# Blocks 3 to 8 of the first network in three pairs, seven products for each gate and value term, sums kept in PSUM

## The chip, the cores and the metric

One core of one Trainium2 chip runs the whole program. The metric is device microseconds of one execution, the median of several. PE (TensorE) does the matmuls, DVE (VectorE), ACT (ScalarE) and POOL (GpSimd) the elementwise work; SP and ACT issue the DMAs. PSUM has eight banks of 128x512 fp32; "bank" always means one of these.

## The reference

Attention in chunks of 64 positions for 8 batches, 8 heads and 576 positions of width 64 gives x of 4608 tokens by 512. Two networks follow:

```python
s = scale * q_c @ k_c.T ; p = exp(s - max(s)) ; x = (p / (sum(p) + 1e-9)) @ v_c
xn = x / sqrt(mean(x * x) + 1e-6) * rms_g
y = (silu(xn @ w_gate) * (xn @ w_val)) @ w_out        # 512 -> 1536 -> 512
h = y @ w_in                                          # 512 -> 2048
out = (h * clip(h + 3, 0, 6) / 6) @ w_out2            # 2048 -> 512
```

## The kernel before

Tokens are worked in nine blocks of N = 512. Every fp32 operand is split into a high part and a remainder (fp32r), and a product of two operands is made of three matmuls (high by high, low by high, high by low). One "term" of 128 output rows over the full depth of 512 is then 12 matmuls of 128x512.

The work is under a manual schedule: each engine runs its instructions in the order in which the code issues them, and waits where a semaphore is not there yet. So an instruction that waits on DVE, ACT or POOL holds all that was issued behind it on that engine, and a DMA that waits for its buffer holds what stands behind it on SP's or ACT's queue.

First network, per block b (loop at L903): for each of the 12 tiles f of 128 hidden rows, `mm_up` makes the gate (12 matmuls, L728, bank GB), ACT makes silu from it (L911), `mm_up` makes the value (bank VB), DVE multiplies (L916), `split_act` casts the high part on ACT (`ah`, L781) and takes the remainder on POOL (`al`, L782), and `mm_down_a` of the tile before (12 matmuls, L752, L753, L755) adds to four banks of y. So the PE order is gate, value, down, 36 matmuls a tile and 432 a block. At the block's end `x_split` makes XH (ACT, L717) and XL (DVE and POOL, L719) of the next block, the last `mm_down_a` runs, and `y_store` (L788 to L790) puts y into DRAM.

Between these steps two hooks put other work, by the position hk (three a tile). `att_hook` runs the attention of block b+1: two units (class Pair) of 256 tokens each with their transposes (L581, L582), scores (L594), max, subtract, exp, sum, normalization on POOL (L630), and so on, then `halve` and `rms` (L692 to L707: squares' mean by two matmuls, square root on ACT with a table load, RECIPROCAL and four multiplies on DVE). `prep_hook` runs `Stash.step`: in each of blocks 1 to 8 it prepares one of eight parts of the second network's weights (raw loads, bit operations L238 to L247 and sums L288 to L291 on DVE, high parts on ACT, remainders on POOL, sixteen 256 KB stores from ACT's queue).

The second network takes block 0 by `mm_up` and blocks 1 to 8 in four pairs by the Strassen-Winograd scheme: seven block products in place of eight, each a `product` of six matmuls (L739) with weight operands streamed from the stash (`Stream.ahead`, L349, 512 KB each) and token operands made by `x_fill` (differences L954, casts L959, remainders L962). Its sums are made outside PSUM: ACT copies a product out (L1027), DVE adds the others (L1030 to L1052).

The change touches the first network's block loop, the hooks, `Stash.step`, `rms`, `x_split` and `product`, and adds an operand preparation and a loader.

## Time and profile before

| what | value |
|---|---|
| median of 3 runs | 1764.86 us (1764.82 to 1765.2) |
| profiled execution, span from first to last instruction | 1762.2 us |
| median less that span | 2.7 us |
| PE busy | 1720.4 us, 98% |
| DVE, ACT, POOL busy | 51%, 37%, 28% |
| matmuls of 128x512 | 7168 |

The page gives the span of the profiled execution and no separate total for it; the runs agree within 0.4 us, so the span and the median differ by what lies around the span. A matmul's busy time overlaps its neighbour's, so the pitch of a run of matmuls is taken from the chain, where pieces stand end to end.

### The profile page before, as it was taken

Reading aid. Unit: us, or ns where it says so; the run is one execution under the profiler, and the core shown is the slowest. Engines: PE = TensorE matmul, PEld = TensorE weight load, DVE = VectorE, ACT = ScalarE, POOL = GpSimd, SP = SyncE. Lnnn points to the kernel's source line nnn. Section 1 sums busy time; section 2 is a strip of 40 time slices with the busy share of each in tenths; the row PEclk is TensorE's granted clock in tenths of the full one; section 3 lists DMA queues with packets and bytes.
Section 4 is the critical chain, followed back from the end, with each engine's and each line's share of the span. In section 5 each row is a group of like instructions: output and inputs, shape, how many; then the busy total and the mean of one; then the engine's idle time right before and its main releaser. Section 6 shows DMA issues by size and latency. Waiting matters only on the chain.

```text
span 1762.2 us, 24680 instructions
## 1 busy us (share of the span) xinstructions
PE 1720.4 (98%) x9664; PEld 1416.8 (80%) x9664; DVE 893.4 (51%) x1202; ACT 644.5 (37%) x971; POOL 488.8 (28%) x360
## 2 busy tenths in 40 slices
PE   5789999999999999999999999999999999999999
PEld 4568788888888888888888888888888888888887
DVE  7996544545455444545542243545554554465440
ACT  5554334333343334334332133333333333343332
POOL 2321332333233232332323232112321321151123
PEclk8889999999999999999999999999999999999999
DMA  9832342423424242343317354544244334424420
GB/s 253 236 85 36 97 108 75 108 64 91 108 76 117 64 106 71 97 108 77 92 51 263 140 204 147 175 143 144 72 167 139 125 111 137 138 92 146 142 67 29
DMA packets 273589, 207.17 MB, mean 118 GB/s; under 512 B 196289, under 2 KB 233153, under 8 KB 273345
## 3 DMA queue, kind: packets, MB, share of 16 engines
q1 hardware_dynamic: 240704, 163.65, 32.4%
q10 hardware_dynamic: 32768, 41.95, 7.2%
q8 instruction: 76, 1.25, 0.3%
q14 instruction: 41, 0.33, 0.1%
HBM read 161.48 MB, written 44.04 MB: 117 GB/s over the span
## 4 chain that ended last, share of the span: by engine, by line
PE 93%; DVE 4%; SPq 1%; POOL 1%; ACT 1%; issue 0%; DMA 0%; DVEq 0%; ACTq 0%
PE PS L728 34%; PE PS L739 17%; PE PS L764 7%; PE PS L761 7%; PE PS L760 7%; PE PS L752 6%; PE PS L753 5%; PE PS L755 5%; PE PS L654 1%; PE PS L594 1%; DVE w L195 1%; PE PS L636 1%; DVE wtmp L175 1%; POOL al L782 1%; DVE wtmp L171 1%; DVE wraw L179 1%
## 5 line engine op out<-in xcount | busy, mean ns | idle before, releaser
L782 POOL TENSOR_TENSOR al<-sg,ah 128x512 fp32r<-128x512 f32 x156 | 215.5, 1381 | 988.6 <-ACT ah L781 685.9
L728 PE MATMUL PS<-XH,w 128*128 128x512 f32 x1728 | 432.3, 393 | 9.3 <-DVE sg L916 4.6
L728 PEld LDWEIGHTS PS<-XH,w 128*128 128x128 f32 x1728 | 326.7, 189 | 79.1 <-DVE sg L916 5.3
L739 PE MATMUL PS<-xo,wq 128*128 128x512 f32 x1344 | 309.2, 389 | 0.0
L739 PEld LDWEIGHTS PS<-xo,wq 128*128 128x128 f32 x1344 | 252.3, 188 | 52.4
L728 PE MATMUL PS<-XL,w 128*128 128x512 f32 x864 | 232.3, 391 | 0.0
L760 PE MATMUL PS<-w,ah 128*128 128x512 f32 x576 | 224.1, 389 | 0.0
L761 PE MATMUL PS<-w,ah 128*128 128x512 f32 x576 | 224.1, 389 | 0.0
L916 DVE TENSOR_TENSOR sg<-sg,PS 128x512 f32<-128x512 f32 x108 | 74.0, 685 | 283.6 <-PE PS L728 274.3
L781 ACT CAST ah<-sg 128x512 fp32r<-128x512 f32 x156 | 96.8, 621 | 272.5 <-DVE sg L916 242.4
L728 PEld LDWEIGHTS PS<-XL,w 128*128 128x128 f32 x864 | 163.0, 189 | 34.7 <-POOL XL L520 0.6
L752 PE MATMUL PS<-ah,w 128*128 128x512 f32 x432 | 174.4, 404 | 1.3 <-ACT ah L781 1.3
L753 PE MATMUL PS<-ah,w 128*128 128x512 f32 x432 | 169.4, 392 | 0.0
L764 PE MATMUL PS<-w,al 128*128 128x512 f32 x576 | 154.3, 389 | 0.0
L911 ACT ACTIVATE sg<-PS 128x512 f32<-128x512 f32 x108 | 64.5, 597 | 227.4 <-PE PS L728 175.3
L761 PEld LDWEIGHTS PS<-w,ah 128*128 128x128 f32 x576 | 108.1, 188 | 22.5
L764 PEld LDWEIGHTS PS<-w,al 128*128 128x128 f32 x576 | 108.1, 188 | 22.4
L760 PEld LDWEIGHTS PS<-w,ah 128*128 128x128 f32 x576 | 108.1, 188 | 22.4
L755 PE MATMUL PS<-al,w 128*128 128x512 f32 x432 | 115.8, 390 | 0.0
L1030 DVE TENSOR_TENSOR u<-u,PS 128x512 f32<-128x512 f32 x32 | 22.0, 687 | 156.8 <-PE PS L739 147.7
L752 PEld LDWEIGHTS PS<-ah,w 128*128 128x128 f32 x432 | 81.5, 189 | 20.0 <-ACT ah L781 1.8
L755 PEld LDWEIGHTS PS<-al,w 128*128 128x128 f32 x432 | 81.3, 188 | 17.3 <-POOL al L782 0.3
(140 smaller groups left out, 1941.1 us busy)
## 6 DMA issues: line engine op xcount, KB each, us to landing
wq<-stash_in SPq DMA_DIRECT2D x152, 512.0 KB, 3.7
yd<-yst SPq DMA_DIRECT2D x18, 512.0 KB, 3.3
sraw<-in_moe_w_in_dram ACTq DMA_DIRECT2D x16, 512.0 KB, 4.9
stash_in<-slo ACTq DMA_DIRECT2D x32, 256.0 KB, 2.7
sraw<-in_moe_w_out_dram ACTq DMA_DIRECT2D x16, 512.0 KB, 5.9
w<-stash_out SPq DMA_DIRECT2D x16, 512.0 KB, 5.1
x<-yd SPq DMA_DIRECT2D x16, 512.0 KB, 5.9
out_dram<-ost SPq DMA_DIRECT2D x16, 512.0 KB, 2.9
```

Source lines behind the costliest of these rows:

```text
L728: nc.tensor.matmul(ps, w(wi, c), xs[c][xi], start=(i == 0), stop=(i == n - 1))
L739: nc.tensor.matmul(PS[:, bank, :], op[:, wi, c * 128:(c + 1) * 128], x[xi][:, c, :], start=(i == 0), stop=(i == 5),)
L752: nc.tensor.matmul(ps, wm[0], a[0], start=first, stop=False)
L753: nc.tensor.matmul(ps, wm[1], a[0], start=False, stop=False)
L755: nc.tensor.matmul(PS[:, YB + m, :], w[:, 0, m * 128:(m + 1) * 128], a[1], start=False, stop=last)
L760: nc.tensor.matmul(PS[:, base + m, :], am, w[:, 0, :], start=first, stop=False)
L761: nc.tensor.matmul(PS[:, base + m, :], am, w[:, 1, :], start=False, stop=False)
L764: nc.tensor.matmul(PS[:, base + m, :], a[1][:, m * 128:(m + 1) * 128], w[:, 0, :], start=False, stop=last)
L781: nc.scalar.copy(hi, t)
L782: nc.gpsimd.tensor_tensor(lo, t, hi.bitcast(F32), op=ALU.subtract)
L911: nc.scalar.activation(s, PS[:, GB, :], AF.Silu)
L916: nc.vector.tensor_tensor(s, s, PS[:, VB, :], op=ALU.mult)
```

## The change

Blocks 0 to 2 keep the gate, value, down order. Blocks 3 to 8 become three pairs p = 0, 1, 2. In a pair, the gate and the value of hidden tiles f = 0..11 are made for both blocks together: six steps i of two tiles, seven operands for each step, each operand used for gate (m = 0) and value (m = 1) by one `product` of six matmuls. That is 84 products, 504 matmuls, where the two blocks took 576. Then 24 `mm_down_a` follow for both blocks. A "tick" is 12 matmuls' worth of steps: two products, or one `mm_down_a`; a pair has 42 and 24 ticks.

The sums of the scheme stay mostly in PSUM: a product starts on a bank that already holds a partial sum (`first=False`). Where one partial sum goes into two results, ACT copies it from bank to bank (L1176, and again at L1183 and L1192). DVE adds one product to an SBUF tile or multiplies; silu runs on ACT; POOL multiplies two of the four gate-value tiles.

Weight operands of the pairs are made once in blocks 1 and 2 by `Operands` (twelve of them, sums on DVE and POOL, high parts on ACT, seven stores of ACT's queue each) and put into DRAM, as are the w_out tiles (`keep_w`). In a pair `Loads.ahead` streams 42 operands and 12 w_out tiles, 512 KB each, six ahead, into the pool `wp`, on SP's queue. Token operands (fourteen high and low tiles) come from `x_ops`: differences and remainders on DVE, casts on ACT.

The hooks are replaced by an agenda: `at(t, fn)` puts a step at tick t. Attention units move ahead (four in each of pairs 0 and 1, none in pair 2), the eight stash parts lie within the three pairs (24 ticks each), `rms` is split into steps with the reciprocal in two halves, and the q, k, v loads are issued at most five a tick.

```diff
+STEPS_P = (
+    (0, ("turn_q",)),
+    (1, ("turn_k",)),
+    (3, ("scores", "top")),
...
+    def at(t, fn, *args, turn=2):
+        agenda[t].append((turn, lambda: fn(*args)))
...
-            t = st_p.tile([128, 1024], U32, tag="st", name="sraw")
+            t = wp.tile([128, 1024], U32, tag="w", name="sraw")
...
+        def whole(self):
+            w = [W[key] for key in self.key]
+            for k_, (t, h) in enumerate(((w[0], 0), (w[0], 1), (w[1], 1))):
+                nc.scalar.dma_start(out=self.d[:, k_, self.m], in_=t.bitcast(F32)[:, :, h * 256:(h + 1) * 256])
+            self.u = [tmp_p.tile([128, 512], F32, tag="tmp", name="ou") for _ in range(2)]
+            for u, t, e in zip(self.u, w, (nc.vector, nc.gpsimd)):
+                e.tensor_tensor(u, t[:, 0, :].bitcast(F32), t[:, 1, :].bitcast(F32), op=ALU.add)
...
+            for d, fn in ((0, self.whole), (1, self.sums), (3, self.high), (3, self.low), (4, self.keep)):
+                at(t0 + d, fn, turn=3)
...
+                    t = wp.tile([128, 2, 2, 256], F32R, tag="w", name="wo")
+                    nc.sync.dma_start(
+                        out=t.bitcast(F32).rearrange("p a b c -> p (a b c)"),
+                        in_=d1[i][:, k_].rearrange("p a b c -> p (a b c)"),
+                    )
...
+        def inv(self, h):
+            r = self.rt[:, h * 256:(h + 1) * 256]
+            nc.vector.reciprocal(r, r)
...
-    def product(bank, op, x):
+    def product(bank, op, x, first=True, last=True):
...
-                    start=(i == 0),
-                    stop=(i == 5),
+                    start=first and i == 0,
+                    stop=last and i == 5,
...
+            (4, (66, 67, 67, 67, 67, 67)),
...
+        for i, t0 in enumerate((6, 33, 58, 86, 112, 134, 153, 172)):
+            stash[i].plan(P0 + t0)
...
+            def lo(j, c, x):
+                nc.vector.tensor_tensor(XO[j][1][:, c, :], x, XO[j][0][:, c, :].bitcast(F32), op=ALU.subtract)
+
+            def diff(p, m):
+                t = tmp_p.tile([128, N], F32, tag="tmp", name="xt")
+                nc.vector.tensor_tensor(t, p, m, op=ALU.subtract)
+                return t
...
-        for b in range(NB):
+        for b in range(3):
...
+        def split_wp(t):
+            w = wp.tile([128, 2, N], F32R, tag="w", name="gs")
+            nc.scalar.copy(w[:, 0, :], t)
+            nc.gpsimd.tensor_tensor(w[:, 1, :], t, w[:, 0, :].bitcast(F32), op=ALU.subtract)
...
+                    product(bk[z][m], loads.t[key][:, m], XO[x], pr in (1, 5), pr in (2, 3, 4))
+                    if m == 1:
+                        loads.t.pop(key)
+                        loads.ahead(1)
+                    if pr == 1 and i == 0:
+                        copy(bank(1, m), bank(0, m))
...
+                    if (pr, m) == (4, 0):
+                        silu(gt(h1, 0), bank(1, 0))
+                        if i < NI:
+                            copy(bank(1, 0), bank(0, 0))
+                    elif (pr, m) == (3, 0):
+                        t = gt(h0, 1)
+                        vec(t, t, bank(4, 0), ALU.add)
+                        later = t
+                    elif (pr, m) == (4, 1):
+                        t = gt(h1, 0)
+                        vec(t, t, bank(1, 1), ALU.mult)
+                        if i < NI:
+                            copy(bank(1, 1), bank(0, 1))
+                    elif (pr, m) == (3, 1):
+                        s = hold.pop("s2")
+                        vec(s, s, bank(4, 1), ALU.add)
+                        t = gt(h0, 1)
+                        nc.gpsimd.tensor_tensor(t, t, s, op=ALU.mult)
+                    elif (pr, m) == (6, 0):
+                        copy(gt(f0, 1), bank(1, 0))
+                    elif (pr, m) == (6, 1):
+                        hold["s2"] = sg_p.tile([128, N], F32, tag="sg", name="s2")
+                        copy(hold["s2"], bank(1, 1))
+                    elif (pr, m) == (2, 0):
+                        silu(gt(f0, 0), bank(0, 0))
+                    elif (pr, m) == (2, 1):
+                        t = gt(f0, 0)
+                        vec(t, t, bank(0, 1), ALU.mult)
+                    elif (pr, m) == (7, 0):
+                        t = gt(f1, 1)
+                        copy(t, bank(1, 0))
+                        vec(t, t, bank(4, 0), ALU.add)
+                        later = t
+                    elif (pr, m) == (7, 1):
+                        s3 = tmp_p.tile([128, N], F32, tag="tmp", name="s3")
+                        copy(s3, bank(1, 1))
+                        vec(s3, s3, bank(4, 1), ALU.add)
+                        t = gt(f1, 1)
+                        nc.gpsimd.tensor_tensor(t, t, s3, op=ALU.mult)
...
+                if 0 < n < len(items) - 2:
+                    nx.append(split_wp(gt(items[n + 2][1], items[n + 2][0])))
+                mm_down_a(loads.t[p, "out", f, 0], nx[n], f == 0, f == FA - 1, yb[z])
```

Three places in the order of the engines. First DVE at the end of block 2, where the normalization of block 4 (L704 to L707, now L772 and L781) is the last before the next block. Before:

```order
L916 TENSOR_TENSOR sg<-sg,PS 128x512
L704 RECIPROCAL rt<-rt 128x512
L707 SCALAR_TENSOR_TENSOR xf<-xf,g_sb,rt 128x512 x4
L916 TENSOR_TENSOR sg<-sg,PS 128x512
L719 TENSOR_TENSOR XL<-xf,XH 128x512 x2
L789 COPY yst<-PS 128x512 x2
```

In the changed kernel, with xt and xu the token operands' differences and their split tiles, and xw the normalized block 3:

```order
L1104 TENSOR_TENSOR sg<-sg,PS 128x512
L772 RECIPROCAL rt<-rt 128x256 x2
L781 SCALAR_TENSOR_TENSOR xf<-xf,g_sb,rt 128x512 x4
L1033 TENSOR_TENSOR xt<-xf,xw 128x512
L1033 TENSOR_TENSOR xt<-xf,xt 128x512
L1029 TENSOR_TENSOR xu<-xt,xu 128x512
L1033 TENSOR_TENSOR xt<-xw,xt 128x512
L1104 TENSOR_TENSOR sg<-sg,PS 128x512
L1029 TENSOR_TENSOR xu<-xt,xu 128x512
L1033 TENSOR_TENSOR xt<-xf,xw 128x512
```

The four norms stand ahead of the block's last multiply as before; now a difference, another, a remainder and a third difference of `x_ops` stand between them and that multiply, and the two remainders XL behind it are gone.

ACT at the same place. Before:

```order
L703 ACT_TABLE_LOAD
L703 ACTIVATE rt<-PS,eps 128x512
L911 ACT_TABLE_LOAD
L911 ACTIVATE sg<-PS 128x512
L781 CAST ah<-sg 128x512
L717 CAST XH<-xf 128x512 x4
L788 COPY yst<-PS 128x512 x2
```

And in the changed kernel:

```order
L768 ACT_TABLE_LOAD
L768 ACTIVATE rt<-PS,eps 128x512
L1026 CAST xu<-xt 128x512
L1100 ACT_TABLE_LOAD
L1100 ACTIVATE sg<-PS 128x512
L1026 CAST xu<-xt 128x512
L874 CAST ah<-sg 128x512
L1026 CAST xu<-xt 128x512 x2
L881 COPY yst<-PS 128x512 x2
L1176 COPY PS<-PS 128x512 x2
```

A cast of the first difference now stands between the square root and the silu (with its table load) of the block's last tile, and after y two bank-to-bank copies (PS<-PS) follow.

PE where blocks 3 and 4 begin. Before, a block's start:

```order
L755 MATMUL PS<-al,w 128x512 x4
L728 MATMUL PS<-XH,w 128x512 x8
L728 MATMUL PS<-XL,w 128x512 x4
L728 MATMUL PS<-XH,w 128x512 x8
L728 MATMUL PS<-XL,w 128x512 x4
L728 MATMUL PS<-XH,w 128x512 x8
L728 MATMUL PS<-XL,w 128x512 x4
L728 MATMUL PS<-XH,w 128x512 x8
L728 MATMUL PS<-XL,w 128x512 x4
L594 MATMUL PS<-kT,qT 64x64 x32
L752 MATMUL PS<-ah,w 128x512
L753 MATMUL PS<-ah,w 128x512
```

And the start of the first pair, wo being the streamed operands:

```order
L848 MATMUL PS<-al,w 128x512 x4
L831 MATMUL PS<-xu,wo 128x512 x48
L655 MATMUL PS<-kT,qT 64x64 x32
L831 MATMUL PS<-xu,wo 128x512 x84
L697 MATMUL PS<-ident,p 128x128 x8
L831 MATMUL PS<-xu,wo 128x512 x24
L715 MATMUL PS<-qT,v 64x64 x32
L831 MATMUL PS<-xu,wo 128x512 x60
L655 MATMUL PS<-kT,qT 64x64 x32
```

The gate, value and down runs of the tiles give way to long runs of products, with the attention of later blocks between them; in the third pair all 504 stand in one row.

## Rows read from the trace of the kernel before

**Rows 1.** The page's head and its first part: busy us of each engine (share of the span).

```profile
span 1762.2 us, 24680 instructions
PE 1720.4 (98%) x9664; PEld 1416.8 (80%) x9664; DVE 893.4 (51%) x1202; ACT 644.5 (37%) x971; POOL 488.8 (28%) x360
```

**Rows 2.** Windows: start:end, length, busy us of five engines (instructions), PEclk, DMA share, GB/s.

```profile
64.00:66.00 2.00, 1.73 (x5) 1.39 (x6) 2.00 (x5) 1.37 (x3) 0.00 (x0) 0.68 0.90 264
70.00:123.00 53.00, 45.36 (x298) 35.31 (x297) 49.28 (x86) 28.04 (x45) 16.58 (x7) 0.90 0.58 154
176.00:182.00 6.00, 4.67 (x21) 3.52 (x21) 4.79 (x6) 3.65 (x7) 3.30 (x3) 1.00 0.05 11
182.00:287.00 105.00, 105.00 (x705) 86.52 (x704) 52.27 (x61) 39.44 (x56) 31.18 (x23) 1.00 0.36 91
930.00:940.00 10.00, 10.00 (x46) 8.28 (x45) 2.34 (x5) 1.84 (x4) 1.28 (x1) 1.00 0.96 355
```

**Rows 3.** The chain of waits, two of its pieces: start us, us, engine, tile, line, matmuls.

```profile
181.70 10.88 PE PS L728 x48
1268.22 19.04 PE PS L739 x84
```

**Rows 4.** Waits of PE after 50 us: the line, what it waited for, us, times, longest.

```profile
PE PS L728 <- DVE sg L916: 4.6, 2, 3.8
PE PS L728 <- ACT sg L911: 2.7, 2, 2.4
...
PE PS L701 <- DVE sqh L693: 0.4, 1, 0.4
```

**Rows 5.** Timeline of PE after a wait: start us, us, engine, line, tiles, count, [idle before].

```profile
64.27 3.43 PE L728 MATMUL PS<-XH,w 128*128 128x512 f32 x8 [2.38 <-ACT sg L911]
68.72 2.00 PE L728 MATMUL PS<-XH,w 128*128 128x512 f32 x8
```

**Rows 6.** Timeline at a block's end, DVE, ACT and PE (columns as in rows 5).

```profile
701.02 1.28 ACT L911 ACT_TABLE_LOAD   x1 [2.56 <-PE PS L728]
701.88 2.74 DVE L707 SCALAR_TENSOR_TENSOR xf<-xf,g_sb,rt 128x512 f32<-128x512 f32 x4
...
704.54 0.68 DVE L916 TENSOR_TENSOR sg<-sg,PS 128x512 f32<-128x512 f32 x1
...
706.22 0.39 PE L752 MATMUL PS<-ah,w 128*128 128x512 f32 x1
```

**Rows 7.** Groups by line: line, engine, operation, tiles, shapes, count | busy us, mean ns | idle before.

```profile
L1027 ACT COPY u<-PS 128x512 f32<-128x512 f32 x32 | 18.8, 586 | 44.6 <-PE PS L739 44.6
L782 POOL TENSOR_TENSOR al<-sg,ah 128x512 fp32r<-128x512 f32 x156 | 215.5, 1381 | 988.6 <-ACT ah L781 685.9 <-PE PS L764 295.8 <-DMA q<-in_q_dram 6.9
L962 DVE TENSOR_TENSOR xo<-xt,xo 128x512 fp32r<-128x512 f32 x32 | 35.9, 1144 | 5.4 <-ACT xo L959 5.4
L247 DVE SCALAR_TENSOR_TENSOR sraw<-sraw,sc 128x512 uint32<-128x512 uint32 x32 | 33.2, 1038 | 1.1
L1030 DVE TENSOR_TENSOR u<-u,PS 128x512 f32<-128x512 f32 x32 | 22.0, 687 | 156.8 <-PE PS L739 147.7 <-ACT u L1027 9.1
```

**Rows 8.** DVE beside POOL: the same view for two pairs of one shape, and a timeline.

```profile
L288 DVE TENSOR_TENSOR sraw<-sraw 128x256 f32<-128x256 f32 x8 | 11.2, 1405 | 0.3
L290 DVE TENSOR_TENSOR sraw<-sraw 128x256 f32<-128x256 f32 x8 | 3.3, 413 | 0.0
...
777.01 1.97 POOL L630 TENSOR_TENSOR p<-p,rs 128x1024 f32<-128x1024 f32 x1 [0.40 <-DVE rs L625]
777.25 2.01 DVE L239 TENSOR_SCALAR sc<-sc 128x512 uint32<-128x512 uint32 x1
```

**Rows 9.** DMA issues (KB each, median us to landing), and ACT's waits for one.

```profile
wq<-stash_in SPq DMA_DIRECT2D x152, 512.0 KB, 3.7
sraw<-in_moe_w_out_dram ACTq DMA_DIRECT2D x16, 512.0 KB, 5.9
...
ACT sg L911 <- DMA stash_in<-slo: 32.6, 7, 5.6
```

More of the change, by code (lines that the diff above doesn't have):

```diff
@@ L754, in mm_down_a @@
         for m in range(KD):
[L755 removed]
+            nc.tensor.matmul(PS[:, banks[m], :], w[:, 0, m * 128:(m + 1) * 128], a[1], start=False, stop=last)
     def mm_down_b(w, a, first, last, in_turn=False, base=YB):
@@ L836, in fused_kernel, with until, attend, plan_unit @@
         xf.pop(0)
-        nxt = Pair(N // TP)
-        parts = nxt.parts_qk()
-        state = {"att": nxt, "parts": parts}
+        unit = [Pair(i) for i in range(NPR)]
+        supply = deque()
+        ready = set()
         def some(n):
-            for _ in range(n):
-                if next(state["parts"], True):
-                    return
+            while n > 0 and supply:
+                if next(supply[0][1], True):
+                    ready.add(supply.popleft()[0])
+                else:
+                    n -= 1
+        def until(key):
+            while key not in ready:
+                some(1)
+        def attend(i, st):
+            u = unit[i]
+            if st == "turn_q":
+                until(("qk", i))
+            elif st == "values":
+                until(("v", i))
+            u.run(st)
+            if i + 1 < NPR:
+                if st == "turn_k":
+                    supply.append((("qk", i + 1), unit[i + 1].parts_qk()))
+                elif st == "values":
+                    supply.append((("v", i + 1), unit[i + 1].parts_v()))
+        def plan_unit(i, t0):
+            for d, steps in STEPS if t0 < P0 else STEPS_P:
+                for st in steps:
+                    at(t0 + d, attend, i, st, turn=0 if st == "squares" else 2)
+        supply.append((("qk", 2), unit[2].parts_qk()))
         before = -1
@@ L883, in prep_hook @@
[L883 to L897 removed]
+        supply.append((("v", 2), unit[2].parts_v()))
@@ new lines, in go @@
+        def go(steps, n):
+            for _ in range(n):
+                if next(steps, True):
+                    return
+        fills = {p: x_ops(3 + 2 * p) for p in range(3)}
+        for p, t0 in ((0, 60), (1, P0 + PAIR - 14), (2, P0 + 2 * PAIR - 14)):
+            for t in range(t0, t0 + 20):
+                at(t, go, fills[p], 2 if p == 0 and t > 71 or p and t in (t0 + 9, t0 + 10) else 1)
+            for t in range(6):
+                at((66 if p == 0 else P0 + p * PAIR - 8) + t, loads.ahead, 1)
@@ L899, in fused_kernel, with prep_hook @@
+        def prep_hook(hk):
+            if not prep_a.done():
+                if hk in STEPS_A:
+                    prep_a.step()
+                prep_a.fill(36)
         order = [(i, k_) for i in range(NQ) for k_ in (0, 2, 3)]
@@ L923, in fused_kernel @@
-                att_hook(b, hk)
-                prep_hook(b, hk)
-                hk += 1
+                for third in range(3):
+                    if third == 1:
+                        mm_up(VB, whole(W["val", f]), xs)
+                        nc.vector.tensor_tensor(s, s, PS[:, VB, :], op=ALU.mult)
+                        a = split_act(s)
+                    elif third == 2 and prev is not None:
+                        mm_down_a(W["out", f - 1], prev, f == 1, False)
+                    tick()
+                    if b == 0:
+                        prep_hook(hk)
+                    hk += 1
@@ L965, in x_fill @@
                     yield
-        def go(steps, n):
-            for _ in range(n):
-                if next(steps, True):
-                    return
         def g_tile(f):
```

439 lines of the change are left out of this document (285 added, 154 removed).

## The prediction, made before the changed kernel ran

> **What bounds the kernel now.** I read the page's head first [rows 1]: PE is busy 1720.4 of 1762.2 us, no other engine more than 51%. A share over the whole span can hide stages with another limit, so next come the windows by stage [rows 2]. From 182 to 287 us, one block's period, PE is busy 105.00 of 105.00 us at a granted clock of 1.00 (the 2.4 GHz level), with DVE at 52.27, ACT at 39.44, POOL at 31.18 and the DMA engines at 0.36: this is PE's stage and nothing else's. From 70 to 123 us, the end of the first block, it is different: DVE is busy 49.28 of 53.00 us and PE 45.36. The waits of PE confirm it [rows 4]: after 50 us there are eight kinds, from 4.6 us down to 0.4, 15.1 us together, and all lie before 182 us. So from there to the end a matmul taken away is time taken away, as long as nothing else comes late; and the question is what the change brings that may come late.
>
> The pitch of a matmul comes from the chain [rows 3], where pieces stand end to end: 48 of 128x512 in 10.88 us and, in the second network's products, 84 in 19.04 us, both 0.2267 us each. The new products are of that second kind: weights just streamed, six matmuls to a bank. I take the same pitch for them.
>
> The profiled span is 1762.2 us and the median of the runs 1764.86, so 2.7 us lie around the span; I make the sum on the span's stages and add the difference at the end, which is the same as starting from 1764.86.
>
> **What is taken away.** The order of PE counts 7168 matmuls of 128x512 before and 6952 after: 216 fewer. The attention's matmuls are unchanged. By the scheme: gate and value of a pair's two blocks took 2 x 288 = 576, now 504, and three pairs make 3 x 72 = 216. At 0.2267 us: 216 x 0.2267 = **-49.0 us**. All of it lies in stages where PE was busy throughout. The floor is 1764.9 - 49.0 = 1715.9.
>
> **What is added, engine by engine, in the pairs.** A pair is 792 matmuls, 179.5 us, and in pairs 0 and 1 about 13 us of attention on PE: 193 us.
> - DVE. Two blocks of before carried 2 x 52.27 = 104.5 us [rows 2]. Out go 24 value multiplies at about 0.69 (the PSUM addition L1030 has 0.687 [rows 7]) = 16.5 and four remainders XL, some 6 us (a group too small for a row here). In come 36 PSUM operations at 0.687 = 24.7; fourteen remainders at 1.144 [rows 7] = 16.0; eight differences, at most that each, some 7; and two thirds of a stash part more, 2.67 for two. A part is four runs of the groups from L238 to L247 (the last 1.038 [rows 7]; about 3.0 together) and the four sums (1.405, 1.4, 0.413, 0.4 [rows 8]), 15.6 us, so 10.4. Together 140 of 193 us, 73%. In pair 2 no attention runs, and it is about half of that.
> - ACT. 36 copies and 24 silus a pair at about 0.6 (L1027: 0.586 [rows 7]) take the place of 24 silus; with casts and table loads it stays under 60%.
> - POOL. 24 remainders and 12 multiplies at 1.38 [rows 7] = 50 us, the stash's remainders some 22 and the attention's normalization 4 x 2 = 8: 80 of 193, 41%.
> - DMA. Attention and stash of one block kept the engines at 0.36 over 105 us [rows 2], 37.8 us of full use. A pair carries two of these and two thirds of a stash part (4.2 MB), and 54 streamed tiles of 512 KB, 28.3 MB. At the best rate that the trace shows, 355 GB/s at a share of 0.96 [rows 2], the streamed tiles take 80 us and the extra stash 12: 75.6 + 80 + 12 = 168 of 193 us, 87%.
>
> No engine is over its time, so the average says PE still bounds. What costs is order.
>
> **Where PE will wait: the end of block 2.** Before, the block's last tile was in time [rows 6]: the norms ran from 701.88 for 2.74 us, the multiply followed at 704.54, and the last down began at 706.22 without a wait, the table load and silu having run from 701.02. Now a cast on ACT of the first difference stands ahead of that table load, and the difference comes after the norms. Walked on the same times: norms end at 704.6, difference 705.3, cast 705.9, table load 1.28 to 707.2, silu 707.8, multiply 708.5, cast of ah 709.1. PE wants ah at 706.2, so it waits 2.9 us. Behind that instruction stand, on PE, the last down and the first pair's products.
>
> A wait has a second price. After a wait of 2.38 us [rows 5] eight matmuls took 3.43 us, against 2.00 a little later, and the four behind them 0.3 more: 1.8 us in addition, the granted clock being 0.68 in that window [rows 2] (between the levels of 1.2 and 2.4 GHz). After the wait of 1.33 us, between 176 and 182 us, it stayed at 1.00 [rows 2]. So I count 1.8 us for waits from about 2 us on, and nothing for those under 1.3. The end of block 2: 2.9 + 1.8 = **+4.7**, from 0 (if the cast is ready sooner) to 7.
>
> **Blocks 0 to 2.** In blocks 1 and 2 DVE had 104.5 us in 210. Two stash parts leave (31); twelve operand preparations come, each an addition and a remainder at 1.14 and four sums of 3.6 together, 5.9 each or 71; and about 14 us of attention from later blocks. That makes 158 of some 216 us, 73%, beside a POOL that works too. At two places attention, normalization and operand sums meet. The multiply of the tile that feeds PE has 4 to 5 us of slack there, and I count +1 (0 to 3) in the middle and +1 (0 to 2) at the first block's end, where two attention steps go ahead of the casts of XH. The first block is DVE's stage, and its attention is issued in another order; I take no change there, with 3 us on either side.
>
> **Inside the pairs.** Nothing in the trace of before shows a product waiting for a bank that DVE or ACT has to read or fill in time. In a step a bank is reused 2.7 us (12 matmuls) after the reading operation may start; that takes 0.7 us, so 2.0 us are free on DVE, and about 3.5 on ACT for a copy from bank to bank. Such a copy has no row of its own; the nearest is L1027, PSUM to SBUF, 0.586 us [rows 7]. Two DVE instructions of 1.04 ahead, as L247 [rows 7], or one that waits for POOL, as L239 did for 2.01 [rows 8], use up the 2.0 us. At the other end, nothing: the second network's products ran without a wait behind similar sums. Nearest to the pairs is that second network, with less on DVE. I take +5 for the three pairs, from 0 to 20: about five waits of 1 us, no drop of the clock.
>
> The sum: 1764.9 - 49.0 + 4.7 + 2 + 5 = **1727.6**, and I say **1727**. The main case runs from 1716 (its floor) to 1737.
>
> **A rule that speaks against it.** L239 took 2.01 us beside a POOL instruction of 1.97 that began at 777.01 [rows 8], more than twice its mean of 0.774; L288 takes 1405 ns and L290, of the same shape, 413, and POOL is at work on the stash's remainders when the first of them run. So DVE and POOL hold each other up. The Trainium skill, page "SBUF — State Buffer", section "SBUF: two separate sides", says why: one pair of SBUF ports is an exclusive lock between them for a DVE operation with two SBUF inputs, and the loser waits for the whole instruction. The trace agrees by those two pairs of rows.
>
> **The rivals.**
> 1. *DVE and POOL exclude each other where both are full.* In pair 0's down ticks (65 us) `split_wp` gives POOL one remainder a tick and the stash adds its own, about 36 us, while DVE has about 42 us of two-input work (stash, token operands of the next pair, attention). If they never overlap, 78 us of work lie in 65: 13 us late at the border to pair 1, and about as much at the next. The next pair's operands come late, PE waits 8 to 13 us at each of two borders and starts again at half clock (2 to 4 us), some 20 to 32 in all above the main case's lower part: 1741 to 1755. For it: [rows 8]. Against it: the mean durations that gave 73% already hold such waits. By the rule of the Trainium skill just cited this is the case to expect in the down ticks. I give it 0.2.
> 2. *The streamed operands come late.* Pair 0 issues all 54 tiles in its first 48 ticks, where the DMA use is nearer 90%, with six tiles (16 us) ahead; q, k, v and raw weights share the engines, and raw tiles take 5.9 us to land against 3.7 [rows 9]. ACT waited 32.6 us in seven waits for the stash's stores [rows 9], and now ACT's queue also fills the banks. If each of pairs 0 and 1 loses 8 us so: 1727 + 16 = 1743, from 1735 to 1760. Against it: from 930 to 940 us PE was busy 10.00 of 10.00 with the DMA share at 0.96 [rows 2]. I give it 0.15.
> 3. *Slower.* In each of the fifteen full steps (five in each pair) one bank is not free in time and PE waits 2.4 us or more, which takes the clock down too: 15 x (2.4 + 1.8) = 63 us, 1715.9 + 63 = 1779. It decides from 49 / 15 = 3.3 us a step. For it: DVE's order is strict, and a stash or attention instruction stands ahead of most PSUM additions. Against it: the 2.0 us are free on top of a queue at 73%. 0.05.
> 4. *No waits worth counting, or gains in the first block:* 1712 to 1716. 0.07.
>
> That the change does less than it says is ruled out by the count of matmuls.
>
> **How the numbers follow.** Main case 0.5 (1716 to 1737), rival 1 0.2, rival 2 0.15, rival 3 0.05, rival 4 0.07, and 0.03 for a loss that just eats the gain. The predicted time is the main case's, 1727. The range has to hold 8 in 10: from 1714 to 1752 it takes in the main case, about half of rival 4 and most of rivals 1 and 2, with some 0.15 left out. A measurement of this kernel can tell about 0.2% (3.5 us) from no change; faster than 1761.3: 0.92; within: 0.03; slower: 0.05.
>
> **What would show it.** Right: PE busy near 1671 us; rows L831 of 24 matmuls in 5.44 us; one wait of about 3 us near the last `mm_down_a` of block 2, on ACT's ah, and clock under 1.00 behind it; few waits over 1 us in the pairs. Rival 1: waits of PE at the pairs' beginnings on xu or on gs, and DVE rows there of 1.5 to 2 us beside POOL. Rival 2: waits on wo or wd tiles from SP's queue. Rival 3: a wait at the same product of each step, on the DVE additions or ACT copies, and windows of the pairs at a clock near 0.7. Wrong altogether: a pitch of the products over 0.23 us without a wait ahead of it.

## The result and the profile after

The changed kernel takes 1781.23 us (median of four runs, 1777.24 to 1786.1), the kernel before 1764.84 on the same chip: a ratio of 1.0094, with an interval of 1.0077 to 1.0111. It is slower by 16 us, where the prediction had 1727 and a range that ended at 1752. The profiled execution is the run of 1777.24 us; its span is 1775.5 us. The head, first part and chain's first line of its page (they answer to [rows 1]):

```profile
span 1775.5 us, 25261 instructions
PE 1687.8 (95%) x9448; PEld 1376.1 (78%) x9448; DVE 985.3 (55%) x1372; ACT 724.0 (41%) x1119; POOL 551.9 (31%) x408
PE 73%; DMA 9%; DVE 8%; SPq 4%; ACT 2%; issue 2%; POOL 1%; ACTq 0%; DVEq 0%; POOLq 0%
```

PE has 9448 instructions where it had 9664, 216 fewer, so the matmuls did go; its busy time fell by 32.6 us. But the chain that ended last, which was PE's to 93%, now has 9% of DMA, 8% of DVE and 4% of SP's queue in it. The windows tell where (columns as in [rows 2]): blocks 0 to 2, then the pairs 0, 1 and 2.

```profile
56.10:412.60 356.50, 336.85 (x2392) 269.34 (x2393) 250.45 (x363) 165.07 (x234) 114.68 (x75) 0.98 0.56 158
412.60:637.50 224.90, 206.35 (x1341) 164.74 (x1341) 128.18 (x161) 102.20 (x156) 74.92 (x53) 0.96 0.74 217
637.50:849.50 212.00, 199.53 (x1342) 160.73 (x1341) 127.73 (x162) 103.82 (x158) 77.96 (x55) 0.99 0.74 230
849.50:1030.60 181.10, 180.09 (x793) 148.46 (x792) 87.11 (x117) 76.16 (x132) 79.61 (x58) 1.00 0.87 311
```

Pair 2, with no attention, needs 181.1 us for its 179.5 us of matmuls. Pairs 0 and 1 need 224.9 and 212.0 where 193 were worked out: PE stands idle for 18.5 and 12.5 us, and in pair 0 the mean granted clock of 0.96 costs some 9 more (an estimate: 0.04 of 224.9). Set against the floor of the prediction (49.0 us less than before), the profiled span is 62.3 us too long: 1.8 before the first block, 11.1 in blocks 0 to 2 (356.5 against 338.4 before, with two attention units, 7 us, taken in from later blocks), and 49 in the pairs (618.0 against 625.2 for blocks 3 to 8 before, less the two units and the 49.0). The second network takes what it took.

The waits of PE in pairs 0 and 1 (columns as in [rows 4]):

```profile
PE PS L831 <- DMA wo<-ops: 13.9, 8, 3.9
PE PS L845 <- ACT gs L1123: 4.2, 3, 2.2
PE PS L845 <- DVE gu L1128: 2.8, 2, 2.2
PE PS L831 <- ACT gu L1199: 2.7, 1, 2.7
PE PS L655 <- DVE kT L643: 2.7, 1, 2.7
```

The first is the one with no row before: products waiting for a streamed operand. The chain around the longest of these waits, from 454 to 500 us (start, length, what; the pieces left out are short):

```profile
454.76 0.39 SPq L409
...
455.20 7.08 DMA wo<-ops
...
462.30 0.47 SPq L634
...
462.81 0.62 SPq L634
...
463.48 0.62 SPq L634
...
464.14 0.60 SPq L409
...
464.78 6.48 DMA wo<-ops
...
474.82 0.61 SPq L409
...
475.48 5.24 DMA wo<-ops
...
482.57 4.73 DMA wo<-ops
...
487.32 5.77 DMA sraw<-in_moe_w_out_dram
...
495.84 4.04 DMA wo<-ops
```

This is a chain without a computing engine in it: an operand lands (7.08 us), only then SP issues three v loads, then the next operand, which lands 6.48 us later, and so on; at 487.32 a raw weight load of ACT's queue is a link in SP's chain. The order of SP's instructions with what each waits for says why. Eight rows of pair 0:

```
547 L409 DMA wo<-ops_134 128x1024 [waits DMAHW2_49,PE_49]
548 L623 DMA q<-in_q_dram 32x6x32 [waits DMAHW4_49]
549 L623 DMA q<-in_q_dram 32x6x32 [waits DMAHW5_49]
550 L623 DMA q<-in_q_dram 32x6x32 [waits DMAHW6_49]
551 L623 DMA q<-in_q_dram 32x6x32 [waits DMAHW7_49]
552 L619 DMA k<-in_k_dram 32x4x32 [waits DMAHW0_49,DVE_49]
553 L619 DMA k<-in_k_dram 32x4x32 [waits DMAHW1_49]
554 L619 DMA k<-in_k_dram 32x4x32 [waits DMAHW2_49]
```

The program gives every DMA one of eight completion semaphores (DMAHW0 to DMAHW7), in turn, and a DMA waits for the one that last had its semaphore, the eighth before it. The turn runs over both queues: DMAHW3 is missing after the first row because a DMA of ACT took it. I call these the eight places. A DMA of 16 KB takes a place like one of 512 KB, and the issuing engine, which works in order, stands while it waits for one. On ACT that holds up the copies and casts behind it. ACT's timeline in pair 0's down ticks:

```profile
562.44 0.37 ACTq L283 DMA_DIRECT2D stash_in<-sc  x1
564.32 0.41 ACTq L283 DMA_DIRECT2D stash_in<-slo  x1
564.77 0.62 ACT L1123 CAST gs<-gu 128x512 fp32r<-128x512 f32 x1 [8.72 <-DMA wd<-keep_out]
```

A cast of gs for a coming `mm_down_a` stood 8.72 us behind two stores of the stash, the second of which waited for the place of a w_out tile of SP's queue. PE had not come to that operand yet. Some 20 us later it had (two rows of ACT's timeline, one of PE's):

```profile
586.54 0.37 ACTq L234 DMA_DIRECT2D sraw<-in_moe_w_out_dram  x1
586.95 0.62 ACT L1123 CAST gs<-gu 128x512 fp32r<-128x512 f32 x1 [2.63 <-DMA q<-in_q_dram]
587.62 0.51 PE L845 MATMUL PS<-gs,wd 128*128 128x512 f32 x1 [2.25 <-ACT gs L1123]
```

A raw load on ACT's queue got its place when a q load of SP's had landed; the cast behind it was late by that, and PE waited 2.25 us for the cast. So two kinds of waits come from the places: products that wait for an operand, and matmuls that wait for ACT.

Per pair the DMA view gives packets, bytes and rate. The first line is pair 0 of the changed kernel (318 issues), the second pair 2 (126), the third pair 0 of the experiment that is told next (106 issues):

```profile
DMA packets 62390, 48.73 MB, mean 217 GB/s; under 512 B 46016, under 2 KB 53411, under 8 KB 62371
```

```profile
DMA packets 23533, 56.27 MB, mean 311 GB/s; under 512 B 2016, under 2 KB 11232, under 8 KB 23392
```

```profile
DMA packets 59040, 48.72 MB, mean 246 GB/s; under 512 B 42640, under 2 KB 50064, under 8 KB 59024
```

Pair 2 moved more bytes, at 311 GB/s in place of 217, and lost 1.6 us.

### The profile page after: what moved, and what is told of

It is laid out like the page before. It is cut to its first block, busy times and chain, and to the rows that moved or that the text cites. A ratio compares the mean times of both kernels' runs of the same rounds, so it can differ in the third digit from the quotient of the medians.

```text
span 1775.5 us, 25261 instructions
## 1 busy us (share of the span) xinstructions
PE 1687.8 (95%) x9448; PEld 1376.1 (78%) x9448; DVE 985.3 (55%) x1372; ACT 724.0 (41%) x1119; POOL 551.9 (31%) x408
## 4 chain that ended last, share of the span: by engine, by line
PE 73%; DMA 9%; DVE 8%; SPq 4%; ACT 2%; issue 2%; POOL 1%; ACTq 0%; DVEq 0%; POOLq 0%
PE PS L831 30%; PE PS L820 8%; PE PS L853 7%; PE PS L854 7%; PE PS L857 7%; DMA wo<-ops 3%; PE PS L845 3%; PE PS L848 3%; PE PS L846 3%; SPq L623 2%; DVE w L194 1%; DMA v<-in_v_dram 1%; DMA wraw<-in_moe_w_out_dram 1%; PE PS L715 1%; DMA k<-in_k_dram 1%
## 5 line engine op out<-in xcount | busy, mean ns | idle before, releaser
L831 PE MATMUL PS<-xu,wo 128*128 128x512 f32 x1512 | 356.9, 395 | 20.0 <-DMA wo<-ops 13.9
L831 PEld LDWEIGHTS PS<-xu,wo 128*128 128x128 f32 x1512 | 284.0, 190 | 86.0 <-DMA wo<-ops 9.4
L875 POOL TENSOR_TENSOR al<-sg,ah 128x512 fp32r<-128x512 f32 x84 | 120.5, 1434 | 582.4 <-PE PS L857 294.2
L820 PE MATMUL PS<-XH,w 128*128 128x512 f32 x576 | 150.5, 403 | 11.3 <-DVE sg L1104 5.5
L820 PEld LDWEIGHTS PS<-XH,w 128*128 128x128 f32 x576 | 109.5, 193 | 39.6 <-DVE sg L1104 6.9
L845 PE MATMUL PS<-gs,wd 128*128 128x512 f32 x288 | 115.5, 401 | 9.2 <-ACT gs L1123 4.2
L846 PE MATMUL PS<-gs,wd 128*128 128x512 f32 x288 | 113.4, 394 | 0.0
L1124 POOL TENSOR_TENSOR gs<-gu,gs 128x512 fp32r<-128x512 f32 x60 | 84.3, 1420 | 46.8 <-ACT gs L1123 41.5
L874 ACT CAST ah<-sg 128x512 fp32r<-128x512 f32 x84 | 52.2, 621 | 98.6 <-DVE sg L1104 69.8
L1128 DVE TENSOR_TENSOR gu<-gu,PS 128x512 f32<-128x512 f32 x60 | 40.9, 683 | 72.7 <-PE PS L831 34.3
L820 PE MATMUL PS<-XL,w 128*128 128x512 f32 x288 | 79.2, 397 | 0.0
L848 PE MATMUL PS<-gs,wd 128*128 128x512 f32 x288 | 78.5, 395 | 0.1
```

The lines of the kernel that those rows point to most:

```text
L820: nc.tensor.matmul(ps, w(wi, c), xs[c][xi], start=(i == 0), stop=(i == n - 1))
L831: nc.tensor.matmul(PS[:, bank, :], op[:, wi, c * 128:(c + 1) * 128], x[xi][:, c, :], start=first and i == 0, stop=last and i == 5, skip_gr ...
L845: nc.tensor.matmul(ps, wm[0], a[0], start=first, stop=False)
L846: nc.tensor.matmul(ps, wm[1], a[0], start=False, stop=False)
L848: nc.tensor.matmul(PS[:, banks[m], :], w[:, 0, m * 128:(m + 1) * 128], a[1], start=False, stop=last)
L874: nc.scalar.copy(hi, t)
```

## The experiments

Theory A: the eight places are the limit, so the number of DMAs counts and not their bytes. Theory B: the DMA engines' bandwidth. Theory C: DVE and POOL hold each other up (rival 1 of the prediction). The diffs are against the changed kernel; a time in brackets behind a median is the range of its runs. Times of pairs come from one profiled execution of each kernel, and the four runs of the changed kernel lie within 9 us, so a few us in a pair tell nothing by themselves.

**Fewer DMAs, the same bytes (e1_few).**

```diff
+            if self.i >= 10:
+                for dst, src in ((self.q, q), (self.k, k)):
+                    rows = src.rearrange("b h s d -> (b h s) d")[(self.i - 2) * 2048:(self.i - 2) * 2048 + 4096, 0:32]
+                    nc.sync.dma_start(
+                        out=dst.rearrange("p (x f) -> p x f", f=32), in_=rows.rearrange("(p x) f -> p x f", x=32)
+                    )
```

> The q, k and v of attention units 10 to 17 are loaded by one DMA each in place of some 52 a unit, with the same bytes (512 KB each) and the same 128 or 256 byte pieces; the rows are not the right ones, so the attention of blocks 5 to 8 works on wrong values. Theory A (the places: a DMA from SP's or ACT's queue is issued only when the DMA issued eight before it has landed, so many small issues hold up the streamed operands): pairs 0 and 1 fall from 225 and 212 us to 193 to 203 each, waits for wo nearly gone, total 1738 to 1750. Theory B (bandwidth of the DMA engines): the bytes are the same, so the pairs stay within 5 us, total 1775 to 1785. Theory C (DVE and POOL hold each other up): unchanged as well, 1775 to 1785.

1739.0 us (1737.79 to 1740.08); ratio to the kernel before 0.9854 (0.9837 to 0.987). Pairs 0, 1 and 2:

```profile
414.20:612.10 197.90, 195.53 (x1341) 160.01 (x1340) 130.05 (x160) 102.13 (x156) 75.13 (x53) 1.00 0.82 246
612.10:809.90 197.80, 195.62 (x1342) 160.03 (x1341) 130.09 (x162) 103.88 (x158) 77.95 (x55) 1.00 0.79 246
809.90:991.00 181.10, 180.08 (x793) 148.47 (x792) 87.07 (x117) 76.20 (x132) 79.95 (x58) 1.00 0.88 311
```

197.9 and 197.8 us, at a clock of 1.00, with the same 48.7 MB in pair 0. The landing of an operand even became longer (7.0 us in the median in pair 0, against 5.6) and did no harm, since few DMAs stood behind it. A holds, B and C fall for the greater part of the loss. That C falls is seen best in pair 0's down ticks, from the first down to the next pair's first product. The first line is the changed kernel, the second e1_few, with the same arithmetic on DVE and POOL:

```profile
551.00:637.50 86.50, 76.20 (x426) 59.87 (x427) 53.94 (x58) 35.34 (x56) 45.59 (x32) 0.94 0.66 197
542.70:612.10 69.40, 69.40 (x430) 57.19 (x427) 50.47 (x53) 33.14 (x52) 41.70 (x30) 1.00 0.70 209
```

Of the 27 us that pair 0 gained, 17 lie there, and PE does not wait there any more.

**More DMAs, the same bytes (e11_split).**

```diff
-                    nc.sync.dma_start(
-                        out=t.bitcast(F32).rearrange("p a b c -> p (a b c)"),
+                    for h in range(2):
+                        nc.sync.dma_start(
+                            out=t.bitcast(F32).rearrange("p a b c -> p (a b c)")[:, h * 512:(h + 1) * 512],
```

> Each streamed operand wo is loaded by two DMAs of 256 KB in place of one of 512 KB: the same bytes, 42 DMAs more in each pair. Theory A: pairs 0 and 1 are slower by 5 to 25 us each, pair 2 (no q, k, v there) by under 3, total 1790 to 1825; a gain from the shorter landing of the halves would speak against the count alone. Theory B: same bytes, total 1772 to 1787.

1797.09 us (1793.63 to 1801.42). Pairs 0, 1 and 2 took 233.1, 217.9 and 181.2 us: 8 and 6 more in the two that carry q, k and v, nothing in the third, although that one too has 42 DMAs more. The number counts only where the places are used up. In the runs so far the loss of a pair above its 193 us goes with the DMAs of SP and ACT counted in its window: 5 us at 106 (pair 0 of e1_few), 19 at 242 (pair 1 of the changed kernel), 25 at 284 (pair 1 here), 32 at 318 (pair 0 of the changed kernel), 40 at 360 (pair 0 here).

**The stash's arithmetic left out (e5_noarith).** With it goes one ACT operation (Abs); the casts on ACT, the loads and the stores stay.

```diff
         def within(self):
-            self.c = tmp_p.tile([128, 512], U32, tag="tmp", name="sc")
...
+            pass
```

> The stash's bit operations and sums on DVE and its remainders on POOL are left out (the second network works on wrong weights); its loads, its casts on ACT and its stores stay, the same bytes and count. Theory A and B: the pairs lose what they lost, total 1770 to 1785, waits for wo stay near 14 us. Theory C: DVE and POOL have 40 and 20 us a pair less, the excess of pairs 0 and 1 goes down by half or more, total 1735 to 1755.

1781.58 us (1774.03 to 1781.95): the same as the changed kernel, though DVE and POOL lost their stash work. Pairs 0 and 1 took 225.1 and 209.3 us by the starts of their products, pair 2 179.5, its floor; so the stash's part in C is worth 0 to 3 us a pair. What the other work of DVE and POOL costs PE is bounded by e1_few, where it all runs and pairs 0 and 1 are within 5 us of 193.

**The small loads spread (e7_rate3).**

```diff
-            some(8 if t < 0 else 5)
+            some(8 if t < 0 else 5 if t < P0 else 3)
```

> In the pairs at most three q, k, v loads are issued in a tick in place of five; count and bytes are the same. Theory A (eight places in turn for all DMAs of SP's and ACT's queues): the streamed operands stand behind three issues in place of five, so the waits for wo fall by a third to two thirds from 14 us and the total by 5 to 15 us, to 1766 to 1776; less, if what counts is the total number of DMAs in a pair (some 315 in 66 ticks), which stays. Theory B (bandwidth): a smoother load may gain 0 to 5 us.

1780.23 us (1773.2 to 1781.8): no change. The waits of PE in pairs 0 and 1 are what tells:

```profile
PE PS L655 <- DVE kT L643: 26.1, 4, 13.7
...
PE PS L831 <- DMA wo<-ops: 0.5, 1, 0.5
```

The 13.9 us for operands went down to 0.5, and the scores now wait 26.1 us for a kT whose k came late. Who goes first can be chosen, and the total stays, as it would with a fixed rate of DMAs. My expectation for A had its alternative in the last clause, and that was the one; B, with 0 to 5 us, allowed the same, so this run does not part the two.

**The operands on ACT's queue (e16_wo_act).**

```diff
-                    nc.sync.dma_start(
+                    nc.scalar.dma_start(
                         out=t.bitcast(F32).rearrange("p a b c -> p (a b c)"),
```

> The 126 streamed operands are issued from ACT's queue, in place of SP's; bytes, count and the turn over the eight places stay. If the cause is that they stand behind the small loads on SP's own queue (its order and its 0.44 us an issue), the waits for wo fall to under 5 us and the total to 1750 to 1768. If the cause is the eight places, taken in turn by both queues, wo still waits for the small loads before it, and now ACT's copies and casts stand behind it: total 1780 to 1830, with PE's waits moved to ACT's gs, gu and PS tiles.

1803.33 us (1800.57 to 1807.44). The waits of PE in pairs 0 and 1:

```profile
PE PS L831 <- ACT PS L1183: 12.0, 3, 5.8
PE PS L831 <- ACT gu L1199: 7.1, 3, 3.2
...
PE PS L845 <- ACT gs L1123: 5.4, 4, 3.3
```

No wait for wo is left in the list, and ACT's copies, among them the bank-to-bank seeds L1183, come late in its place. The total and the engine that is late are those of the second branch of the expectation; that wo would still be waited for was wrong. So it was not SP's own order alone: the places are shared, and whoever issues stands.

One rival was not parted from A. SP needs time of its own for each issue, whatever the places do. Two rows of SP's timeline in pair 0 of the changed kernel, without a wait in them:

```profile
425.19 2.55 SPq L623 DMA_DIRECT2D q<-in_q_dram  x5
427.84 0.39 SPq L409 DMA_DIRECT2D wo<-ops  x1
```

Five loads and an operand take SP 3.0 us, more than a tick of 2.72. Summed over pair 0, SP's 282 issues took 134.8 of its 224.9 us, and 47 us went in waits for a landing; the chain holds 79 us of DMAs under way there and 29 us of SP's queue. e1_few and e18_pe_turn (below) take both away together (61 and 77 us of issues in pair 0). That the places hold the engines up is shown; how the loss divides between them and SP's own time is not.

**DMAs on POOL's queue, which has other completion semaphores (e6_pool, e8_stash_pool, e9_rate3_pool, e14_half_pool, e13_stores_pool, e12_both_pool).** Four of them change the engine name in the issue of one kind of DMA; e9_rate3_pool joins e8_stash_pool with e7_rate3, and e12_both_pool joins e14_half_pool with e13_stores_pool. e6_pool's edit is

```diff
-                    nc.sync.dma_start(
+                    nc.gpsimd.dma_start(
                         out=t.bitcast(F32).rearrange("p a b c -> p (a b c)"),
```

> The 126 streamed operands wo are issued from POOL's queue, which has other completion semaphores, with the same bytes and count. Theory A: the streamed operands no longer stand behind the q, k, v issues; the waits for wo vanish and pairs 0 and 1 lose half of their excess or more, total 1745 to 1765 (POOL's own work for each issue may give some back). Theory B: the same bytes at the same times, total 1775 to 1785, waits for wo stay near 14 us. Theory C: POOL gets more to do, so it is the same or slower, 1778 to 1800.

> The stash's raw loads and stores in the pairs are issued from POOL's queue in place of ACT's; bytes and count are the same. Theory A, with ACT's queue as its second half (ACT's copies and casts stand behind a DMA issue that waits until an SP DMA has landed): ACT's waits for a DMA go, and SP's DMAs have the eight places to themselves; waits of PE for ACT's gs, gu and PS tiles fall from some 11 us to under 4, the waits for wo by a third or more, the total to 1745 to 1765. Theory B: unchanged, 1775 to 1785.

> Both edits together: at most three q, k, v loads a tick, the stash's DMAs on POOL's queue. Theory A: 1738 to 1758, faster than the kernel before. Theory B: 1772 to 1785.

> In the 42 up ticks of pairs 0 and 1 every second q, k, v load is issued from POOL's queue, which takes its turn on other completion semaphores; all data are the right ones. Theory A: the eight places of SP and ACT carry some 60 DMAs fewer in a pair (318 to about 255), so the excess of pairs 0 and 1 (32 and 19 us) falls by a third to two thirds, and POOL has time in these ticks: total 1752 to 1768. Theory B: 1775 to 1785. If POOL's own waits take the place: over 1785.

> Only the stash's stores (16 of 20 DMAs of a part) are issued from POOL's queue; its raw loads, which wait for a buffer, stay on ACT's. If the blocked raw loads were what cost 23 us in pair 2 of the kernel with both on POOL, pair 2 comes back to 181 to 186 us, pairs 0 and 1 to 200 to 213, total 1755 to 1770. If POOL in the down ticks has no room for any issue, pair 2 stays over 195 and the total over 1780.

> Both: every second q, k, v load of the up ticks and the stash's stores on POOL's queue. Theory A: about 210 DMAs a pair are left on the eight places, pairs 0 and 1 at 195 to 208 us, total 1742 to 1760, faster than the kernel before. If POOL becomes the late one, over 1765.

In all six the total that A gave was missed. 1791.64, 1796.12, 1792.82, 1775.96, 1790.53 and 1804.94 us, in the order of the names above; only e14_half_pool is (by 5 us) below the changed kernel, with a ratio to the kernel before of 1.0051 (1.0038 to 1.0064), and its runs spread from 1766.3 to 1779.69. Part of what A says was seen: with the stash on POOL, pair 0 went from 225 to 212 us. In e6_pool the waits for wo are gone, but ACT came late, as in e16_wo_act; pair 0 took 226.8 us, with some 40 DMAs fewer on the eight places, so the count alone does not give the time:

```profile
PE PS L831 <- ACT PS L1183: 12.4, 3, 6.3
```

Where the stash or the small loads went to POOL, it works in order too, and what stands behind an issue there came late in turn: in e8_stash_pool pair 2 went from 181 to 204 us, PE waiting 7.6 us for POOL's gs at once; in e14_half_pool, in pairs 0 and 1,

```profile
PE PS L705 <- POOL p L699: 20.1, 3, 8.0
```

the transposes waited for the attention's normalization on POOL. That POOL's instructions are held by the places of its own queue and by the buffers that its loads wait for is what I read from these waits; it was not tried apart, and an issue takes POOL's own time as well (twelve stores 9.2 us in pair 2 of e13_stores_pool). The Trainium skill, page "DMA: Bandwidth & Descriptors", section "Rules for kernel authors", holds that spreading DMAs over the issuing engines brings no bandwidth and saves issue time only. These six agree as far as they go: five were slower than the changed kernel and one was faster by 5 us.

**The right data in fewer DMAs, two ways (e17_turned, e18_pe_turn).** In the first, sixteen copies from DRAM to DRAM in blocks 1 and 2 lay q and k down so that a unit's load needs two DMAs a run:

```diff
+        for n in range(16):
+            at(2 + 4 * n, turn_rows, n // 2 % 2, 4 + n // 4, n % 2, turn=5)
```

> The right data with fewer DMAs: in blocks 1 and 2 sixteen DRAM to DRAM copies (0.3 MB each, one every four ticks) lay the rows of q and k of the last four batches down with the 32 token rows outermost, so that units 10 to 17 load q and k by two DMAs a batch run each (1 KB pieces) in place of 16 to 24 (128 byte pieces); v as before. A pair has about 180 DMAs in place of 318. Theory A (places): pairs 0 and 1 at 195 to 205 us, total 1733 to 1752, faster than the kernel before. If the sixteen copies disturb blocks 1 and 2 (they land late and hold up places there), these lose up to 10 us more. Theory B (bandwidth): more bytes than before in all, 1778 to 1795.

1810.82 us (1809.52 to 1816.62). The pairs did what A says, 202.5 and 197.9 us; blocks 0 to 2 took 425.3 us in place of 356.5, and there PE waited for this:

```profile
PE PS L676 <- DVE kT L664: 58.4, 4, 20.4
```

The copies moved 576 KB each, not the 0.3 MB of the expectation, and landed after 5.8 us (k) and 6.9 us (q) in the median. That they held up the q and k of the units there, which stand behind them on SP's queue, is read from the order and these waits; it was not tried apart. I had 10 us for it and it cost 69.

In the second, q and k of units 10 to 17 are loaded as they lie and PE turns them, ACT copies them out of PSUM in place of DVE's transposes, and units 12 and 16 begin a tick later:

```diff
+            for a in range(NP):
+                for t in range(2):
+                    c = a % 2 * 256 + t * 128
+                    nc.tensor.transpose(
+                        PS[:, ATT + a // 2, c:c + 128], x[:, t * 512 + a * 128:t * 512 + (a + 1) * 128], ident
+                    )
+            nc.scalar.copy(out.rearrange("p (o n) -> p o n", o=2), PS[:, ATT:ATT + 2, :])
```

> For units 10 to 17 (the ones of the pairs) q and k are loaded as they lie, token rows on the partitions, by two to four DMAs a unit each in place of 16 to 24, and turned by PE (16 transposes of 128x128 a unit, 1.74 us by the 0.87 us of eight in the trace before) and two ACT copies of 1.0 us in place of DVE's two transposes; the data are the right ones. Theory A (places): a pair has some 170 DMAs in place of 318, pairs 0 and 1 come to 193 + 7 (PE's own transposes) + 3 to 8, that is 203 to 208 us, total 1750 to 1764, at or below the kernel before. Theory B: the bytes are the same, pairs at 225 to 235 us, total over 1780.

1752.62 us (1748.44 to 1753.82), ratio to the kernel before 0.9928 (0.9915 to 0.994): faster than both. Pairs 0, 1 and 2:

```profile
415.90:620.70 204.80, 202.53 (x1405) 166.74 (x1404) 122.55 (x152) 109.79 (x164) 75.38 (x53) 1.00 0.73 238
620.70:824.30 203.60, 202.39 (x1406) 166.79 (x1405) 119.39 (x154) 111.48 (x166) 77.85 (x55) 1.00 0.73 239
824.30:1005.60 181.30, 180.28 (x794) 148.51 (x793) 86.42 (x117) 76.17 (x133) 79.98 (x58) 1.00 0.87 310
```

204.8 and 203.6 us, 193 and 7 of PE's own transposes and 4 to 5 of the rest, and a clock of 1.00. Most of the pairs' loss is taken back with the right data.

**The end of block 2 (e4_border, e19_both).** The edit puts the token operands' first differences behind the block's last silu and multiply:

```diff
-                at(t, go, fills[p], 2 if p == 0 and t > 71 or p and t in (t0 + 9, t0 + 10) else 1)
+                if p or t not in (68, 69):
+                    at(t, go, fills[p], 3 if p == 0 and t == 70 else 2 if p == 0 and t > 71 or p and t in (t0 + 9, t0 + 10) else 1)
```

> At the end of block 2 the first token operands' differences, casts and remainders are moved behind the last silu and multiply. The walk of the prediction: the wait of 2.85 us of PE for ah at the end of block 2 goes, and a wait of 0 to 2 us for a token operand may come in the first products; the total falls by 1 to 3 us, within the spread of the runs of this kernel (1777 to 1786).

1786.15 us (1784.82 to 1789.02), 5 above the changed kernel and not 1 to 3 below; the intervals of the two ratios (1.0106 to 1.0136, and 1.0077 to 1.0111) still touch. The wait itself went from 2.85 to 0.2 us, with 1.0 us at the first products, but pair 0 took 233 us in place of 225 in the profiled runs. That an edit elsewhere shifts which DMA stands behind which is a guess that I did not follow further; with the DMAs out of the way the edit was made again, on e18_pe_turn:

> The kernel whose q and k of units 10 to 17 are turned by PE, with the first token operands' differences behind block 2's last multiply as well. With the DMAs out of the way the local change should show in the total: the wait of 2.85 us at the end of block 2 goes to 0.2, 1.0 us comes in the first products, so 1 to 3 us less than 1752.6: 1749.6 to 1751.6. If the total moves by more than 4 us either way, the order of the DMAs behind it has changed the pairs.

1749.38 us (1748.01 to 1750.54), ratio 0.9909 (0.9895 to 0.9922), 3.2 below e18_pe_turn by the medians. The runs and the intervals of the two overlap, so a gain in the total is not shown; the wait of PE for ah is down to 0.2 us here too. This is the best of the kernels here, 16 us under the one before.

## Why the prediction was wrong

- *What bounds the kernel, and the gain.* Right. 216 matmuls went, at the pitch taken from the chain: pair 2, where nothing else interferes, took 181.1 us for 179.5.
- *The end of block 2.* The walk gave a wait of 2.9 us for ah; the trace has it. PE's timeline of the changed kernel:

```profile
409.80 0.50 PE L845 MATMUL PS<-ah,w 128*128 128x512 f32 x1 [2.85 <-ACT ah L874]
```

  The walk's order is the trace's: difference, cast, table load, silu, multiply, cast of ah. The 1.8 us for the clock did not come: from 409 to 416 us the granted clock is 1.00 (its row stands at the end). The rule "1.8 us from about 2 us on" rested on one wait in a stage where PE had been idle much more besides; the wait's own length does not decide it alone.
- *Blocks 0 to 2 besides.* +2 were taken; 11.1 less the 2.85 are some 8. The waits of PE there (those over 0.15 us) add up to 19.5 us, before to 11.8, so 4.8 of the 8 are new waits: the largest is 2.14 us for qT in block 1, where the prediction had +1 for a multiply, and the rest are waits up to 1.2 us at the second border and at multiplies. The other 3 are not traced to a wait.
- *Inside the pairs: the step that failed.* +5 us, 0 to 20, stood there, as five waits of 1 us and no drop of the clock; it was 49, with 31 us of waits in pairs 0 and 1 and half clock behind some of them. I counted the time of DVE, ACT and POOL, and of the DMA engines by bytes, and each had room, rightly: without the stash's arithmetic the time is the same (e5_noarith), and with the same bytes in fewer DMAs most of the loss is gone (e1_few). What I did not count was the number of DMAs against the waits that the order of SP and ACT shows for each one, nor SP's own time for them. The count was to be had before the run: 318 issues in a pair, up to six of SP's in an up tick and ACT's besides, with eight places. What eight places give depends on the time to land, and that I had only for the large DMAs, 3.7 to 5.9 us [rows 9]. In pair 0 of the changed kernel:

```profile
wo<-ops SPq DMA_DIRECT2D x42, 512.0 KB, 5.6
q<-in_q_dram SPq DMA_DIRECT2D x40, 16.0 KB, 4.1
k<-in_k_dram SPq DMA_DIRECT2D x32, 32.0 KB, 2.1
```

  All 318 took 4.0 us in the mean, so eight places would allow 5.4 in a tick of 2.72; SP by itself, at 0.48 us an issue, 5.7. SP's six and ACT's were more than either. What was issued in the up ticks of pair 0 is 4.1 in a tick (209 in 138.4 us), with 6.2 of the eight places in use in the mean. A place in its turn is waited for even where another is free, so the division is an upper bound.
- *Rival 1* (DVE and POOL, 0.2) is not what happened. By the rule of the Trainium skill cited with it, the down ticks should have been late for it. Pair 0's were late, 86.5 us; but they took 83.9 without the stash's arithmetic (e5_noarith), and 69.4 with all of it and fewer DMAs (e1_few). Of the two pairs of rows that the prediction takes as agreement, L288 fits the rule as cited; L239 reads a single tile, and the cited case is an operation with two SBUF inputs.
- *Rival 2* (operands late, 0.15) named the place, the line and the rows, and priced it at 8 us a pair, by bandwidth; pairs 0 and 1 lost 32 and 19, of which PE's waits for wo are 13.9. Its counterargument, PE busy with the DMA share at 0.96 from 930 to 940 us [rows 2], was true of large DMAs and says nothing of many small ones. The row of ACT waiting 32.6 us for a DMA [rows 9] was the hint: no data are waited for there. In the trace before, for one of these seven waits, a raw load of ACT's was issued at 340.19 us, when a q load of SP's with the same semaphore had landed at 340.17, and the silu stood behind it.
- *Rival 3* (slower) came out in its sign by another mechanism.

## What to carry to other kernels

Count DMAs, not only bytes: see in the order what each DMA's issue waits for, and set the number asked for in a stretch against the places divided by the time to land, and against the issuing engine's own time (0.48 us an issue on SP here). A stream that is added to a queue full of small loads is held by them, and moving it to another engine's queue moved the wait to an engine that computes; loading data as they lie and turning them on an engine with room took two thirds of these small loads away and won. And a stage without the suspected cause (pair 2) is an experiment that the trace already holds.

## What was not expected of the hardware

- The landing time of an operand hardly mattered (5.6 us in the changed kernel, 7.0 in e1_few), the number of DMAs did: pair 0 at 217 GB/s with 318 issues lost 32 us, at 246 GB/s with 106 issues and the same bytes 5.
- A wait of 2.85 us (at 409.80) left the granted clock at 1.00, while one of 2.38 us before [rows 5] was followed by half speed; between 550 and 575 us, with two waits of 2.18 and 2.67 us, the clock was 0.81:

```profile
409.00:416.00 7.00, 6.20 (x27) 5.16 (x28) 7.00 (x10) 3.83 (x7) 1.63 (x1) 1.00 0.28 111
550.00:575.00 25.00, 19.66 (x183) 15.33 (x174) 13.58 (x17) 8.48 (x14) 13.54 (x10) 0.81 0.67 199
```
